# Score products of an attention and MLP kernel on four 64x64 corners of TensorE, in plain fp32 for all pairs

## The chip, the core and the metric

The kernel runs on one core of a Trainium2 chip. A core has five engines that work side by side, each with a queue of its own: TensorE (PE) for matmuls, VectorE (DVE), ScalarE (ACT), GpSimd (POOL), and SyncE (SP), which here only issues DMAs. PE reads its operands from SBUF, 128 partitions of on-chip memory, and writes to PSUM, also of 128 partitions; DVE and ACT read PSUM. The metric is the device time of one launch in microseconds.

## What is computed

Causal attention over 4 batches of 12 heads with 448 rows of 64, and on its result a two-layer MLP with 1792 tokens, 768 and 2048 wide:

```python
scores = q @ k.T / sqrt(64)                   # per head, 448 x 448
scores = np.where(upper_triangle, -1e9, scores)
attn = softmax(scores)
x = (attn @ v), heads side by side            # 1792 x 768
h = x @ w_in                                  # 1792 x 2048
g = np.where(h >= 1, h, np.where(h <= -1, 0, (h + 1) ** 2 / 4))
out = g @ w_out                               # 1792 x 768
```

q and k are large here (a spread of about 3.2), so that the softmax is sensitive to errors in the scores. The weights come as 8-byte floats and are narrowed on the chip.

## The kernel before

**Units of work.** Two heads form a pair: head 0 stands in SBUF partitions 0 to 63 and head 1 in 64 to 127. There are 24 pairs, `n_pair` 0 to 23, six in each batch. The 448 query rows of a head are seven tiles of 64, `i` = 0 to 6; by the causal mask tile `i` needs 64 (i+1) columns of keys.

**One pair.** `prep_pair` loads q and k (tile st) and transposes them on DVE to qs (L713). Scores go to PSUM tiles s (four of 128x512). DVE adds the mask and takes the row minimum of the negated scores (L884), ACT takes the exponential and its sum (L888), POOL or DVE and DVE make the reciprocal (L894 to L899), and one of three engines scales the row (`finish`, L768 to L772). `turn` transposes the rows on PE by a product with an identity (L785, 16 matmuls a pair) and ACT or DVE copies them to pt. PV (L913) multiplies them with v, on two halves of PE's columns, one for each head; its result is split into two rounded parts x (fp32r), which are the input of the first MLP product (L608, three passes: high with high, high with low, low with high).

**Scores, two ways.** Pairs 0 to 4 (`no < FLAT`) take q and k in plain fp32: `flat_scores` gives head 0 the corner of rows 0 to 63 and columns 0 to 63 of PE, head 1 the corner of rows 64 to 127 and columns 64 to 127 (L835, 14 matmuls a pair, of which each stands twice in the trace). Pairs 5 to 23 split q and k into a rounded part and the rest, tiles tt and ks (`copy_alts` L462 to L464, `sub_alts` L471 and L472), and compute in three fp32r passes: `last_scores` for tile 6 with both heads in one product by way of qb, a block diagonal of q (L845, 3 matmuls of 448 columns), and `wide_scores` for two tiles at once, each head on its half of PE's rows (L865, 18 matmuls; its tiles are as wide as the wider of the two).

**What sets the order.** Nothing is in program order. Each step is a task with the engines that may run it and a cost for each; `Plan.solve` ranks the tasks by due times, which `at()` and the tables of `steps_of_plan` give for PE, runs a model of the machine, and then moves tasks about by the seeds in `STEPS`, each of which stands for one random shift. The order of every engine's queue is what that model ends with. Loads of w_in (with their narrowing on ACT and DVE, L491 to L496, and splitting, L462 to L472) lie among the first ten pairs, w_out's after them. At the start PE runs `WARM` = 10 filling matmuls on zeros (L939) whose result nobody reads, and some more while pair 0 waits. After the last pair the second MLP product (L1028) runs alone on PE.

Of the kernel before, what the change touches and what calls it, by code (L numbers as in the profile page):

```python
# [2 lines left out]

# [30 lines left out]
class Task:  # L34
    def __init__(self, alts, prio):
        self.alts, self.prio = alts, prio
        self.deps, self.soft, self.allocs = set(), set(), []
        self.next = []
        self.mode = 0
        self.nom = self.moved = None  # L40
        self.lat = 1.6

# [5 lines left out]
class Plan:  # L48
# [8 lines left out]
    LANES = 8  # L57
    AHEAD = 12.0
# [88 lines left out]
    def solve(self):  # L147
# [4 lines left out]
        for ahead in (22.0,):  # L152
            for pen in (0.4,):
                self.AHEAD, self.PEN = ahead, {"DVE": pen, "ACT": 0.1}
# [29 lines left out]
    )  # L184

    def shake(self, seed):
# [8 lines left out]
        kind = rng.randrange(3)  # L195
# [15 lines left out]
    def run(self, dry=False):  # L211
        for t in self.tasks:
            t.reset()
        free, held, pe = {"SP": 0.56, "DVE": 0.63}, {}, Clock()
# [6 lines left out]
        while left:  # L221
# [21 lines left out]
            for prio, _, s, t in can:  # L243
                e0, c0, _, p0 = t.alts[0]
                c0 = 0.0 if e0 == "PE" else c0
                own = max(s, free.get(e0, 0.0) + queued.get(e0, 0.0), port if p0 else 0.0) + c0
                for a, (e, c, _, p) in enumerate(t.alts):
# [3 lines left out]
                    if a and st + c + queued.get(e, 0.0) + self.PEN.get(e, 0.0) >= own:  # L251
                        continue
                    chosen.setdefault(e, []).append(((st, prio), t, a, st, 0.0 if e == "PE" else c))
                queued[e0] = queued.get(e0, 0.0) + c0
            for e, cands in chosen.items():
                first = min(cands, key=lambda x: x[0])
                limit = first[3] + self.LOOK * first[4]
                key, t, a, st, _ = min((x for x in cands if x[3] <= limit and x[0][1] <= first[0][1]),
                                       key=lambda x: (x[0][1], x[0][0]))
                if best is None or key < best[0]:  # L260
                    best = (key, t, a, st)
# [85 lines left out]
def kernel(  # L347
# [9 lines left out]
    nc = tc.nc  # L357
# [27 lines left out]
    WARM = 10  # L385
# [6 lines left out]
        "tt": 2, "qs": 3, "ks": 2, "vr": 2, "pt": 2,  # L392
        **{f"p{i}": 1 for i in range(NI)}, "qb0": 1, "qb1": 1,
# [19 lines left out]
    open_pools(attn, "tt qs ks vr pt mn su")  # L413
# [17 lines left out]
    mask2 = early.tile([P, 3 * P], F32, name="mask2")  # L431
    nc.gpsimd.memset(mask2, 0.0)
    nc.gpsimd.affine_select(
        out=mask2[:, 2 * P:], in_=mask2[:, 2 * P:], pattern=[[-1, P]], compare_op=ALU.is_ge,
        fill=-1e30, base=0, channel_multiplier=1,
    )
# [6 lines left out]
    qb = [early.tile([P, 2, 2, T], F32R, name=f"qb{n}") for n in range(2)]  # L443
# [196 lines left out]
    S_AT = {6: 0.0, 5: 0.06, 4: 0.25, 3: 0.31, 2: 0.5, 1: 0.58, 0: 0.62}  # L640
# [19 lines left out]
    W_AT, W_T = 0.9, {6: 0.0, 5: 0.3, 4: 1.0, 3: 1.7, 2: 2.4, 0: 3.1}  # L660

    def at(n, kind, i):
        if n >= FLAT:
            t = starts[n] + W_AT
            if kind == "S":
                return starts[n] if i == 6 else t + 1e-4 * (i == 3)
# [8 lines left out]
        last = {6: 5, 5: 5, 4: 3, 3: 3}.get(i, 0)  # L675
        if kind == "T":
            return s_at(last) + LAG_T + 0.01 * (6 - i)
        return s_at(0) + LAG_T + LAG_V
# [6 lines left out]
    QS, KS, VR = {}, {}, {}  # L685
# [6 lines left out]
    def prep_pair(b, p, prio):  # L692
        no = b * HP + p
        flat = no < FLAT
        x = QS[b, p] = [buf("qs", [P, S]) for _ in range(2)]
        nat = []
        for g in range(2):
            t = buf("st", [P, ROW])
            first = None
            for i in range(2):  # L700
                row = (q, k)[g][b, 2 * p + i]
                for z in range(2):
# [3 lines left out]
                             dma(32 * 2 * S * 4, 230.0), 0.465, lat=1.25, early=no == 0, writes=[(t, 2 * i + z)], behind=loads[-1:] if first is None else ())  # L706
# [3 lines left out]
        ks = None if flat else buf("ks", [P, 2, S], F32R)  # L710
        qt = None if flat else buf("tt", [P, 2, S], F32R)
        for g, t in enumerate(nat):
# [4 lines left out]
            if flat:  # L717
                continue
# [5 lines left out]
        if flat:  # L724
            return
        bd, qd = plan.buf(f"qb{no % 2}", lambda: None), qb[no % 2]
        KS[b, p] = qt, ks, bd, qd
        if no in (FLAT, FLAT + 1):
            for z in range(2):
                task([("POOL", pool_ts(2 * T), lambda z=z: nc.gpsimd.memset(  # L730
                    qd[64 * z:64 * z + 64, :, 1 - z].bitcast(F32), 0.0), True)], prio, writes=[(bd, z)])
        for z in range(2):
            a = slice(64 * z, 64 * z + 64)
            task(copy_alts(lambda a=a, z=z: qd[a, :, z], lambda a=a: qt[a, :, S - T:].bitcast(F32), 2 * T, "POOL ACT DVE"),
                 prio, reads=[(qt, 0), (qt, 1)], writes=[(bd, 2 + z)])
# [15 lines left out]
    def pair(b, p, prio):  # L751
        n_pair = b * HP + p
        flat = n_pair < FLAT
        x, vr = QS[b, p], VR[b, p]
        qt, ks, bd, qd = KS.get((b, p), (None,) * 4)
# [4 lines left out]
        wide = [not flat and i < 6 for i in range(NI)]  # L760
        width = [T * ((i | 1 if wide[i] else i) + 1) for i in range(NI)]
# [14 lines left out]
        def turn(ii):  # L776
# [3 lines left out]
            def tr():  # L780
                for m, i in enumerate(ii):
                    for j in range(nb):
                        c = ((1 - m if wide[i] and nt > 1 else m) * nb + j) * P
                        k = min(P, S - j * P)
                        nc.tensor.transpose(t[:k, c:c + P], es[i][:, j * P:j * P + k], ident)  # L785
# [9 lines left out]
            def dst():  # L795
                if wide[lo] and nt > 1:
                    return pt[:, :2].rearrange("p i g q -> p g i q")
                if wide[lo]:
# [308 lines left out]
```

## Time and profile before

| | before |
|---|---|
| median of 3 runs | 633.13 us (631.77 to 633.73) |
| the profiled execution | 630.88 us |
| its span in the profile | 629.1 us |
| PE busy | 607.3 us (97%) |
| DVE busy | 467.3 us (74%) |
| ACT busy | 340.9 us (54%) |
| POOL busy | 208.5 us (33%) |

The profiled execution took 630.88 us, of which 629.1 are the span that the profile shows; 1.8 us lie around it. A busy PE counts from the start of a matmul to the end of its way through the array, and matmuls overlap, so the price of a matmul in a stream is the distance between starts and not its duration. A matmul in plain fp32 stands twice in the trace, as two records.

### The profile page before, as it was taken

To read this page: it belongs to the slowest core of one execution; us is meant where nothing else is said; L and a number is where in the kernel's file an instruction comes from. 1 tells how busy PE (TensorE), PEld (TensorE's weight loads), DVE (VectorE), ACT (ScalarE), POOL (GpSimd) and SP (SyncE) were. 2 spreads that over 40 slices of the span, in tenths; PEclk is the share of its full clock that TensorE was granted. 3 is DMA by queue.
4 is the path that set the end of the run, shared out by engine and by line. 5 is a ranking of instruction groups with operands and counts; after the bars stand their busy time and mean duration, and the time that the engine had idled before them with its cause. 6 is when DMAs were issued, how large, how long until landed. Compare 5 with 4: busy or idle time off the path is not lost.

```text
span 629.1 us, 11519 instructions
## 1 busy us (share of the span) xinstructions
PE 607.3 (97%) x3652; PEld 527.1 (84%) x3652; DVE 467.3 (74%) x1197; ACT 340.9 (54%) x851; POOL 208.5 (33%) x353
## 2 busy tenths in 40 slices
PE   7889999999999999999999999989999999999997
PEld 4455678797789798778798778979999999999997
DVE  4788898979996868976766619998766675665763
ACT  3888896748894546993554826845232322222320
POOL 3657765725661304681142606321101010110110
PEclk9999999999999999999999999999999999999999
DMA  8888789558868877668854119955423233424321
GB/s 212 235 198 214 188 244 278 143 165 244 252 192 272 245 241 228 167 204 244 260 160 162 31 51 324 329 177 191 118 84 118 72 118 83 131 68 118 105 83 64
DMA packets 96589, 110.33 MB, mean 175 GB/s; under 512 B 33552, under 2 KB 86288, under 8 KB 96528
## 3 DMA queue, kind: packets, MB, share of 16 engines
q1 hardware_dynamic: 96336, 109.15, 58.7%
q8 instruction: 29, 0.48, 0.3%
q10 hardware_dynamic: 192, 0.44, 0.2%
q14 instruction: 32, 0.26, 0.1%
HBM read 78.36 MB, written 31.20 MB: 174 GB/s over the span
## 4 chain that ended last, share of the span: by engine, by line
PE 73%; DMA 10%; DVE 7%; ACT 5%; issue 2%; POOL 1%; SPq 1%; ACTq 0%; DVEq 0%; POOLq 0%
PE h L608 21%; PE s L1028 16%; PE h L1028 8%; PE t L1028 8%; PE t L913 6%; DMA w<-in_moe_w_in_dram 6%; PE s L608 5%; PE t L785 5%; PE s L865 3%; ACT e L888 2%; DMA sr<-in_moe_w_out_dram 2%; DMA st<-in_q_dram 1%; DVE vv L621 1%; PE s L845 1%; DVE w L471 1%
## 5 line engine op out<-in xcount | busy, mean ns | idle before, releaser
L608 PE MATMUL h<-x,w 128*128 128x448 f32 x900 | 204.0, 372 | 2.7 <-DVE vv L621 2.2
L608 PEld LDWEIGHTS h<-x,w 128*128 128x128 f32 x900 | 162.3, 188 | 16.4 <-DVE vv L621 4.0
L462 ACT ACTIVATE hl<-z 128x896 fp32r<-128x896 f32 x56 | 53.5, 955 | 135.4 <-DVE z L471 93.9
L1028 PE MATMUL s<-w,hl 128*128 128x384 f32 x534 | 101.6, 335 | 3.1 <-DVE vv L621 3.1
L1028 PEld LDWEIGHTS s<-w,hl 128*128 128x128 f32 x534 | 93.5, 188 | 3.5 <-DVE vv L621 3.4
L888 ACT ACTIVATE e<-s,mn 128x128 f32<-128x128 f32 (+6 forms) x168 | 81.4, 496 | 16.0 <-DVE mn L884 11.8
L471 DVE TENSOR_TENSOR z<-z 128x128 f32<-128x128 f32 x196 | 54.4, 312 | 43.4 <-DMA z<-g_scratch 41.2
L884 DVE CUSTOM_DVE_ANT_0 s<-s,mask 128x128 f32<-128x128 f32 (+5 forms) x168 | 72.5, 468 | 8.9 <-PE s L835 4.9
L471 DVE TENSOR_TENSOR hl<-z,hl 128x896 fp32r<-128x896 f32 x54 | 60.4, 1126 | 15.8 <-ACT hl L462 15.7
L785 PE MATMUL t<-ident,e 128*128 128x128 f32 (+1 forms) x384 | 61.8, 279 | 5.6 <-ACT pt L818 1.8
L472 POOL TENSOR_TENSOR z<-z 128x128 f32<-128x128 f32 x28 | 12.6, 467 | 154.2 <-DMA z<-g_scratch 121.4
L785 PEld LDWEIGHTS t<-ident,e 128*128 128x128 f32 (+1 forms) x384 | 43.4, 139 | 20.5 <-ACT pt L816 3.0
L769 POOL TENSOR_SCALAR e<-e,su 128x256 f32<-128x256 f32 (+5 forms) x95 | 52.3, 556 | 24.0 <-DVE su L899 17.4
L618 ACT ACTIVATE r<-h,half 128x448 f32<-128x448 f32 x50 | 31.5, 635 | 45.9 <-PE h L608 44.4
L713 DVE STREAM_TRANSPOSE qs<-st 128x448 f32<-128x448 f32 x48 | 46.3, 968 | 11.2 <-DMA st<-in_q_dram 7.4
L816 ACT ACTIVATE pt<-t 128x256 f32<-128x256 f32 (+2 forms) x117 | 49.3, 445 | 8.3 <-PE t L785 7.9
L1028 PE MATMUL h<-w,hl 128*128 128x384 f32 x258 | 52.8, 335 | 0.0
L1028 PE MATMUL t<-w,hl 128*128 128x384 f32 x258 | 52.7, 335 | 0.0
L608 PE MATMUL s<-x,w 128*128 128x448 f32 x252 | 52.2, 364 | 0.4 <-DVE vv L621 0.4
L621 DVE TENSOR_TENSOR vv<-h,r 128x448 f32<-128x448 f32 x50 | 31.0, 620 | 26.7 <-ACT r L618 26.5
L913 PE MATMUL t<-pt,vr 128*64 128x448 f32 (+3 forms) x384 | 50.3, 391 | 0.5 <-ACT pt L816 0.4
L608 PEld LDWEIGHTS s<-x,w 128*128 128x128 f32 x252 | 46.9, 188 | 3.8 <-DVE vv L621 0.7
(103 smaller groups left out, 881.2 us busy)
## 6 DMA issues: line engine op xcount, KB each, us to landing
g_scratch<-r SPq DMA_DIRECT2D x64, 224.0 KB, 3.1
z<-g_scratch SPq DMA_DIRECT2D x56, 256.0 KB, 2.9
sr<-in_moe_w_out_dram SPq DMA_DIRECT2D x32, 384.0 KB, 4.4
w<-in_moe_w_in_dram SPq DMA_DIRECT2D x28, 384.0 KB, 4.8
w_scratch<-wn SPq DMA_DIRECT2D x56, 192.0 KB, 3.5
st<-in_q_dram SPq DMA_DIRECT2D x94, 108.0 KB, 3.4
st<-in_k_dram SPq DMA_DIRECT2D x94, 108.0 KB, 3.6
w<-w_scratch SPq DMA_DIRECT2D x50, 192.0 KB, 4.2
```

Source lines behind the costliest of these rows:

```text
L462: "ACT": ("ACT", act(n, 0.04), lambda: nc.scalar.activation(out=dst(), in_=src(), func=ACTF.Copy)),
L471: "DVE": ("DVE", dve(n), lambda: nc.vector.tensor_tensor(out=dst(), in0=x(), in1=y(), op=op), port),
L608: nc.tensor.matmul(out=h[:, :S], lhsT=wi[f][kk // K2][:, a, kk % K2 * P:(kk % K2 + 1) * P], rhs=x[:, c], start=(kk == 0 and n == 0), stop= ...
L621: task([("DVE", dve(S), lambda: nc.vector.tensor_tensor(out=y.tile, in0=h[:, :S], in1=r.tile, op=ALU.max))], g0, reads=[(h, 0), (r, 0)], w ...
L713: task([("DVE", 0.81, lambda g=g, t=t: nc.vector.transpose(out=x[g].tile.rearrange("p (r c) -> p c r", c=C), in_=bands(t[:, :32])))], prio ...
L769: ("POOL", pool_ts(n, 0.09), lambda: nc.gpsimd.tensor_scalar(out=ev(), in0=ev(), scalar1=sc(), scalar2=1.0, op0=ALU.mult, op1=ALU.mult), T ...
L785: nc.tensor.transpose(t[:k, c:c + P], es[i][:, j * P:j * P + k], ident)
L816: nc.scalar.activation(out=dst(), in_=src(), func=ACTF.Copy)
L884: task([("DVE", dve(n) + (0.05 if n < 384 else 0.02), lambda s=s, off=off, n=n, i=i: nc.vector.tensor_tensor_reduce(out=s[:, off:off + n], ...
L888: task([("ACT", act(n, 0.19), lambda s=s, off=off, n=n, i=i: nc.scalar.activation(out=es[i][:, :n], in_=s[:, off:off + n], func=ACTF.Exp, ...
L913: nc.tensor.matmul(out=o[64 * g:64 * g + 64, j * P:S], lhsT=vr[:k, j, g, :], rhs=pt[:k, 7 * j:5 * j + NI, g, :] if j < NJ - 1 else pt[:k, ...
L1028: nc.tensor.matmul(out=acc[x][:, :NO], lhsT=hl[:, a, i * P:(i + 1) * P], rhs=(hi, lo)[c](), start=(f == 0 and n == 0), stop=(f == KF - 2 a ...
```

## The change

All 24 pairs take their scores in plain fp32. `quads` computes a whole pair with 14 matmuls in two tasks, each with two s tiles. In the first s tile head 0 goes to partitions 0 to 63 and head 1 to 64 to 127, as in `flat_scores`; in the second tile they are crossed (`turned_`), so that all four corners of 64x64 are named in turn: head 0 straight, head 1 straight, head 0 crossed, head 1 crossed. Tile 6 (448 columns) is paired with tiles 5 and 0 (384 + 64), tiles 3 and 2 (256 + 192) with 4 and 1 (320 + 128). The crossed tiles are turned back by the transposes, whose identity is rotated by 64 columns for them (`SWAPPED`, `turners`). tt, ks, qb, mask2 and the wide and last products are gone. Around this the planner's costs, due times and seeds are new (`STEPS` has 150 seeds for 101), `qs` has four slots for three, the first two pairs use buffers of x (`head`), and `WARM` is 18.

```diff
-    TURNS_WIDE = ((6,), (5,), (4,), (3,), (2,), (0, 1))
     TURNS = ((6,), (5,), (4,), (2, 3), (0, 1))
     GROUPS = ((6, 5), (4, 3), (2, 1, 0))
-    GROUPS_WIDE = ((6,), (5, 4), (3, 2), (1, 0))
-    FLAT = 5
+    QUADS = ((6,), (5, 0)), ((3, 2), (4, 1))
+    SWAPPED = 5, 4, 1, 0
+    EVEN = 5
-    WARM = 10
+    WARM = 18
-        "tt": 2, "qs": 3, "ks": 2, "vr": 2, "pt": 2,
+        "qs": 4, "vr": 2, "pt": 2,
-    STEPS = (
-        1000008, 1000015, 1000095, 1000120, 1000197, 1000199, 1000222, 1000307, 1000343, 1000359, 1000388,
...
+        5000004, 5000005, 5000008, 5000014, 5000017, 5000026, 5000027, 5000036, 5000038, 5000043, 5000066,
...
-    ident = const.tile([P, P], F32, name="ident")
-    make_identity(nc, ident)
+    ident = const.tile([P, P + T], F32, name="ident")
+    make_identity(nc, ident[:, :P])
+    nc.gpsimd.tensor_copy(out=ident[:, P:], in_=ident[:, :T])
+    turners = ident[:, :P], ident[:, T:]
...
-                        nc.tensor.transpose(t[:k, c:c + P], es[i][:, j * P:j * P + k], ident)
+                        nc.tensor.transpose(t[:k, c:c + P], es[i][:, j * P:j * P + k], turners[i in SWAPPED])
...
-            y = (qt, ks)[g]
-            task(copy_alts(lambda y=y: y[:, 0], lambda g=g: x[g].tile, S, "ACT POOL DVE"),
-                 prio, reads=[(x[g], 0)], writes=[(y, 0)])
-            task(sub_alts(lambda y=y: y[:, 1], lambda g=g: x[g].tile, lambda y=y: y[:, 0].bitcast(F32), S, "DVE POOL"),
-                 prio, reads=[(x[g], 0), (y, 0)], writes=[(y, 1)])
...
+        def quads(slots):
+            ss = [buf("s", [P, 512]) for _ in slots]
+            queues, keys = [], []
+            for turned_, (s, tiles) in enumerate(zip(ss, slots)):
+                off = 0
+                queues.append([])
+                for i in tiles:
+                    place[i] = s, off
+                    keys.append((s, off))
+                    queues[-1].append((s, turned_, i, off))
+                    off += width[i]
+            def qk():
+                for step in zip_longest(*queues):
+                    for s, turned_, i, off in (y for y in step if y):
+                        for g in range(2):
+                            z, o = slice(64 * g, 64 * g + 64), 64 * (g ^ turned_)
+                            nc.tensor.matmul(out=s[o:o + 64, off:off + width[i]], lhsT=x[0][z, i * T:(i + 1) * T],
+                                             rhs=x[1][z, :width[i]], start=True, stop=True)
```

How the order moves, at two places. On SP, at the start, the rows of before (st, x: raw q and k; vr: v; w: raw w_in):

```order
L454 DMA st<-in_q_dram 32x864 x2
L454 DMA st<-in_k_dram 32x864 x2
L454 DMA vr<-in_v_dram 128x4x64 x2
L454 DMA w<-in_moe_w_in_dram 128x3x256
L454 DMA vr<-in_v_dram 128x4x64 x2
L454 DMA w<-in_moe_w_in_dram 128x3x256 x2
L454 DMA st<-in_q_dram 32x864 x2
```

and of the change:

```order
L463 DMA st<-in_q_dram 32x864 x2
L463 DMA st<-in_k_dram 32x864 x2
L463 DMA x<-in_q_dram 32x864 x4
L463 DMA x<-in_k_dram 32x864 x4
L463 DMA vr<-in_v_dram 128x4x64 x2
L463 DMA st<-in_q_dram 32x864 x3
L463 DMA st<-in_k_dram 32x864 x4
L463 DMA st<-in_q_dram 32x864
L463 DMA vr<-in_v_dram 128x4x64 x2
L463 DMA w<-in_moe_w_in_dram 128x3x256 x4
```

The q and k of the second and third pair have moved ahead of the first loads of w_in. On PE, among the pairs of the second batch, where PV of one pair (L913, L868) is followed by scores of a later one; before:

```order
L608 MATMUL h<-x,w 128x448 x60
L913 MATMUL t<-pt,vr 64x448 x2
L913 MATMUL t<-pt,vr 64x320 x2
L913 MATMUL t<-pt,vr 64x192 x2
L913 MATMUL t<-pt,vr 64x64 x2
L865 MATMUL s<-ks,tt 128x384 x6
L865 MATMUL s<-ks,tt 128x128 x6
L865 MATMUL s<-ks,tt 128x256 x6
L608 MATMUL h<-x,w 128x448 x12
L845 MATMUL s<-ks,qb_144 128x448 x3
```

and of the change:

```order
L868 MATMUL t<-pt,vr 64x64 x2
L820 MATMUL s<-qs 64x256 x2
L820 MATMUL s<-qs 64x320 x2
L820 MATMUL s<-qs 64x192 x2
L820 MATMUL s<-qs 64x128 x2
L820 MATMUL s<-qs 64x448 x2
L820 MATMUL s<-qs 64x384 x2
L820 MATMUL s<-qs 64x64 x2
L617 MATMUL h<-x,w 128x448 x15
L768 MATMUL t<-ident,e_130 128x128 x3
```

The wide products after a PV and the last tile's product among the MLP's matmuls have become one run of 14 small matmuls. Over the whole program DVE stands with 1211 instructions for 1197, ACT with 619 for 686, POOL with 247 for 351.

## Rows read from the trace of the kernel before

**Rows 1.** The page: busy time, share of the span and instructions of each engine.

```profile
PE 607.3 (97%) x3652; PEld 527.1 (84%) x3652; DVE 467.3 (74%) x1197; ACT 340.9 (54%) x851; POOL 208.5 (33%) x353
```

**Rows 2.** Stretches: length, busy us of PE, PEld, DVE, ACT, POOL; clock, DMA share, GB/s.

```profile
10.00:75.00 65.00, 58.45 (x418) 35.21 (x416) 52.49 (x181) 52.52 (x169) 40.07 (x73) 1.00 0.81 210
75.00:125.00 50.00, 47.36 (x278) 39.41 (x279) 46.07 (x107) 39.37 (x104) 31.60 (x41) 1.00 0.78 226
125.00:404.00 279.00, 276.77 (x1703) 231.81 (x1702) 213.75 (x578) 177.77 (x489) 112.07 (x187) 1.00 0.67 206
425.00:629.00 204.00, 200.59 (x1156) 200.26 (x1154) 132.03 (x293) 58.12 (x69) 15.80 (x28) 1.00 0.35 104
```

**Rows 3.** The chain of waits by line, from 10 to 125 us and from 125 to 425.

```profile
by line: DMA w<-in_moe_w_in_dram 30.5%; PE t L913 7.1%; PE h L608 6.6%; ACT e L888 4.8%; PE s L835 4.5%; PE t L785 4.3%; DMA st<-in_q_dram 4.1%; issue 3.8%; POOL e L769 3.3%; DVE qs L713 3.2%; ACT wn L491 3.2%; ACT pt L816 3.2%; DMA vr<-in_
...
by line: PE h L608 41.2%; PE s L608 10.1%; PE t L913 9.6%; PE t L785 8.4%; PE s L865 5.3%; DMA sr<-in_moe_w_out_dram 3.3%; issue 2.9%; DVE w L471 2.1%; ACT e L888 2.1%; DVE vv L621 2.0%; PE s L845 2.0%; DVE z L471 1.0%; DVE s L884 0.9%; DMA
```

**Rows 4.** PE's timeline from 208 us: start, us, line, operation, tiles, shapes, count.

```profile
208.19 4.12 PE L913 MATMUL t<-pt,vr 128*64 128x448 f32 x32
212.25 1.49 PE L865 MATMUL s<-ks,tt 64*128 64x384 f32 x18
213.67 0.87 PE L608 MATMUL h<-x,w 128*128 128x448 f32 x3
```

**Rows 5.** PE's timeline around the last tile's product of one pair.

```profile
198.48 0.78 PE L845 MATMUL s<-ks,qb 128*128 128x448 f32 x3
199.10 1.16 PE L608 MATMUL h<-x,w 128*128 128x448 f32 x5
```

**Rows 6.** The chain in order of time: start, us, what; a flat pair's scores, then PV.

```profile
20.91 3.01 PE s L835 x20
23.93 0.43 PE s L835 x4
24.37 1.97 PE t L913 x14
```

**Rows 7.** PE's timeline: two flat matmuls, and flat matmuls beside PV's last product.

```profile
20.84 0.59 PE L835 MATMUL s<-qs 64*64 64x448 f32 x2
...
26.08 0.27 PE L835 MATMUL s<-qs 64*64 64x64 f32 x1
26.17 0.23 PE L913 MATMUL t<-pt,vr 64*64 64x64 f32 x2
```

**Rows 8.** PE's timeline at the start; in brackets the idle time before and its releaser.

```profile
1.44 4.63 PE L939 MATMUL h<-ks 128*128 128x512 f32 x10 [1.44 <-DVE ks L932]
...
8.46 6.11 PE L835 MATMUL s<-qs 64*64 64x448 f32 x28 [2.39 <-DVE qs L713]
```

**Rows 9.** PE's timeline: four transposes and what starts after them.

```profile
161.85 0.62 PE L785 MATMUL t<-ident,e 128*128 128x128 f32 x4
162.40 1.49 PE L865 MATMUL s<-ks,tt 64*128 64x384 f32 x18
```

**Rows 10.** DVE's groups from 10 to 125 us: count, busy us, mean ns, idle before.

```profile
L884 DVE CUSTOM_DVE_ANT_0 s<-s,mask 128x384 f32<-128x384 f32 (+6 forms) x63 | 26.9, 458 | 6.3 <-PE s L835 4.9 <-ACT e L888 1.2 <-ACT qb L462 0.2
L713 DVE STREAM_TRANSPOSE qs<-st 128x448 f32<-128x448 f32 x21 | 20.4, 971 | 4.8 <-DMA st<-in_q_dram 3.4 <-PE s L835 1.0 <-DMA st<-in_k_dram 0.4
L496 DVE SCALAR_TENSOR_TENSOR wn<-w,wn 128x384 uint32<-128x384 uint32 x28 | 17.8, 647 | 0.1
L494 DVE TENSOR_SCALAR wn<-wn 128x384 uint32<-128x384 uint32 x28 | 11.3, 411 | 1.4 <-ACT wn L491 1.4
```

**Rows 11.** Instructions on tile qs: duration min/median/max in ns, first and last start.

```profile
L472 POOL TENSOR_TENSOR tt<-qs,tt x15: 1131/1152/1473, 49.1 to 341.9; 128x448 fp32r<-128x448 f32 x15
L471 DVE TENSOR_TENSOR ks<-qs,ks x14: 605/621/1010, 55.6 to 343.4; 128x448 fp32r<-128x448 f32 x14
```

**Rows 12.** PE's waits from 125 to 404 us: us in total, times, longest.

```profile
PE t L785 <- ACT pt L816: 1.0, 3, 0.5
...
PE t L785 <- ACT e L771: 0.2, 1, 0.2
```

More of the change, by code (lines that the diff above doesn't have):

```diff
@@ L41, in __init__ @@
         self.lat = 1.6
+        self.first = 0
     def reset(self):
@@ L57 @@
     LANES = 8
+    FREE = {"SP": 0.73, "ACT": 0.72, "DVE": 0.9, "POOL": 3.5}
     AHEAD = 12.0
@@ L151, in solve @@
         best = None
-        for ahead in (22.0,):
-            for pen in (0.4,):
-                self.AHEAD, self.PEN = ahead, {"DVE": pen, "ACT": 0.1}
+        for ahead in (14.0,):
+            for pen in (0.1,):
+                self.AHEAD, self.PEN = ahead, {"DVE": pen, "ACT": 0.1, "POOL": 12.0}
                 when = {t: t.nom for t in pe}
@@ L194, in shake @@
         part = rng.choice((0.03, 0.1, 0.3, 1.0))
-        kind = rng.randrange(3)
+        kind = rng.randrange(4)
+        if kind == 3:
+            for t in self.tasks:
+                if a <= t.begin <= z and t.moved is None and len(t.alts) > 1 and rng.random() < part:
+                    t.first = rng.randrange(len(t.alts))
+            return
         if kind == 2:
@@ L257, in run @@
                 limit = first[3] + self.LOOK * first[4]
-                key, t, a, st, _ = min((x for x in cands if x[3] <= limit and x[0][1] <= first[0][1]),
+                _, t, a, st, _, asked = min((x for x in cands if x[3] <= limit and x[0][1] <= first[0][1]),
                                        key=lambda x: (x[0][1], x[0][0]))
+                key = asked, t.prio if t.nom is None else t.nom
                 if best is None or key < best[0]:
@@ L430 @@
         )
[L431 to L436, printed above, removed]
     es = []
@@ L693, in prep_pair @@
         no = b * HP + p
-        flat = no < FLAT
-        x = QS[b, p] = [buf("qs", [P, S]) for _ in range(2)]
+        x = QS[b, p] = [head[2 + g] if no == 0 else buf("qs", [P, S]) for g in range(2)]
         nat = []
         for g in range(2):
-            t = buf("st", [P, ROW])
+            t = head[g] if no == 1 else buf("st", [P, ROW])
             first = None
@@ L705, in prep_pair @@
                              lambda row=row, z=z: bass.AP(row.tensor, row.offset + 32 * z, [[C * D, 32], [1, ROW]]),
-                             dma(32 * 2 * S * 4, 230.0), 0.465, lat=1.25, early=no == 0, writes=[(t, 2 * i + z)], behind=loads[-1:] if first is None else ())
+                             dma(32 * 2 * S * 4, 230.0 if no else 185.0), 0.465, lat=1.25 if no else 1.0, early=no == 0, writes=[(t, 2 * i + z)], behind=loads[-1:] if first is None else ())
                     first = first or one
@@ L759, in pair @@
         eb, done, turned = {}, [], []
-        wide = [not flat and i < 6 for i in range(NI)]
-        width = [T * ((i | 1 if wide[i] else i) + 1) for i in range(NI)]
+        width = [T * (i + 1) for i in range(NI)]
         def finish(i):
@@ L795, in dst @@
             def dst():
-                if wide[lo] and nt > 1:
-                    return pt[:, :2].rearrange("p i g q -> p g i q")
-                if wide[lo]:
-                    return rows(pt[:, lo & ~1:(lo | 1) + 1, 1 - lo % 2], nb)
                 if nt > 1:
@@ L826, in turn @@
                  prio, reads=[(t, 0)], writes=[(pt, i) for i in ii])
-        def flat_scores(i):
-            n, s = width[i], buf("s", [P, 512])
-            place[i] = s, 0
-            def qk():
-                for g in range(2):
-                    z = slice(64 * g, 64 * g + 64)
-                    nc.tensor.matmul(out=s[z, :n], lhsT=x[0][z, i * T:(i + 1) * T], rhs=x[1][z, :n],
-                                     start=True, stop=True)
-            return task([("PE", mm(4 * n, T, T, pair=True), qk)], prio, reads=[(x[0], 0), (x[1], 0)], writes=[(s, 0)]), 1
@@ L871, in pair @@
         place = {}
-        for group in GROUPS if flat else GROUPS_WIDE:
+        for group in GROUPS:
             for i in group:
@@ L903, in pair @@
             done.extend(group)
-            for ii in TURNS if flat else TURNS_WIDE:
+            for ii in TURNS:
                 if ii[0] not in turned and all(i in done for i in ii):
@@ L944 @@
     fill(WARM, -1.0)
+    head = [buf("x", [P, n]) for n in (ROW, ROW, S, S)]
     for b in range(B):
```

97 lines of the change are left out of this document (26 added, 71 removed), and 20 rows, old and new, of the table STEPS.

## The prediction, made before the change was run

> **What bounds the kernel now.** I read the page's busy shares first, then the engines' busy time by stretch, then the chain of waits of the same stretches, and last single matmul rows for prices. TensorE (PE) is busy 97% of the span [rows 1], but that is an average over three stages. In the last one (425 to 629 us, the second MLP product, which the change leaves alone) it is busy 200.6 of 204 us. From 125 to 404 us (pairs 10 to 23 with the first MLP product) it is busy 276.8 of 279. From 10 to 125 us (pairs 0 to 9) it is busy only 105.8 of 115, with VectorE (DVE) at 98.6 of 115, and at 46.1 of 50 from 75 us on, and the DMA engines' share near 0.8 [rows 2]. The chain says the same: from 125 to 425 us PE lines lead it (41% + 10% MLP, 10% PV, 8% transposes, 5% wide scores), from 10 to 125 us loads of w_in lead with 30%, and no PE line passes 8% [rows 3]. So a microsecond taken from PE after 125 us is a microsecond of the end; before 125 us it is worth something only as far as DVE, ACT and the loads follow.
>
> **The score products, the term that matters.** Prices are differences of starts, since the durations overlap. Before, one later pair (5 to 23) has 18 wide matmuls, 212.25 to 213.67 = 1.42 us [rows 4], and 3 of the last tile, 198.48 to 199.10 = 0.62 us [rows 5]: 2.04 us. A flat pair (0 to 4) in plain fp32 on two corners: 24 of its matmuls, that is widths 448 to 128 with 1728 columns, take from 20.91 to 24.37 = 3.46 us, 2.00 ns a column [rows 6]; the whole pair has 1792 columns: 3.6 us. The two corners do run at once: two matmuls of 0.59 us each lie inside 0.59 us [rows 7].
>
> After, each corner streams 448 columns in each of two groups, 896 in all. If four corners keep the pace that two keep, a pair costs 896 x 2.00 = 1.79 us. A second row gives nearly the same: PV runs in plain fp32 on two column halves, and its 32 matmuls (two pairs, 2048 columns) take 208.19 to 212.25 = 4.06 us [rows 4], 1.98 ns a column, 1.78 us. The best uninterrupted flat row (20 matmuls, 1600 columns, 3.01 us [rows 6]) gives 1.69. I take 1.78; the other end is that the corners go two and two, 3.6 us. That four do run at once no row shows. The nearest are two: in PV two column halves read the same rows at full pace, in the flat scores two row halves write the same tile at full pace; and at 26.08 to 26.2 us a corner of the score product streams while both corners of PV's last product are still under way [rows 7], three at once. And in the wide product two row halves write the same partitions of two s tiles at once: its 2 x 2304 columns at the last tile's pace (0.62 us for 1344 columns, 0.46 ns each [rows 5]) would take 2.1 us one after another, and they took 1.42. Each condition of the four corners is thus met somewhere, so I go with four.
>
> Here a rule of the Trainium skill speaks against the change: TensorEngine Tiling (Array Packing), section Gotcha 1: PSUM Pressure, says that different row tiles cannot access the same PSUM bank simultaneously. In the new product both row halves write each s tile. The flat rows did that already and overlapped fully [rows 7], so the trace disagrees for two corners; no run here shows it for four. By the rule the sum would be that of the first rival below.
>
> Saved on PE: later pairs 2.04 - 1.78 = 0.26 (0.35 by the best row), x19 = 4.9 to 6.7 us, of which the 14 pairs after 125 us are 3.6 to 4.9. Pairs 1 to 4: 3.6 - 1.8 = 1.8, x4 = 7.2 us. Entering and leaving the split array is paid once a pair in both kernels (the order keeps the 14 new matmuls of a pair mostly together), so I cost it at nothing; where groups stand apart it costs a few tenths, the 0.17 us by which flat and PV overran their columns.
>
> The first pair ran slower: 28 matmuls in 6.11 us from 8.46 to 14.57, 3.4 ns a column, and the ten filling matmuls before it went every 0.43 us or so (4.63 us for ten), the pace of the 1.2 GHz level, though the clock row reads 1.00 there [rows 2, 8]. PE had stood idle for 2.39 us between them. Now 18 fills reach from 1.44 to about 1.44 + 18 x 0.43 = 9.2 us without that gap. If the pace stays low the pair takes 896 x 3.4 = 3.0 us and ends at 12.2; if the 7.7 us of fills bring the upper level, as the 6 us of scores did before, it takes 1.8 and ends near 10.3. Against 14.57 that is 2.4 to 4.3 us; the 0.7 us of later start is in it. I take 3.
>
> PE work saved in all: 5 + 7 + 3 = 15 us (14.4 to 18.1).
>
> **What of it reaches the end.** After 125 us nearly all: 4 us (3.6 to 4.9). Before 125 us PE saves about 1.5 (five later pairs) + 7.2 + 3 = 11.7 us, and what is late next is DVE. Each pair needs seven mask-and-minimum passes on DVE (63 of them, nine pairs, took 26.9 us: 3.0 a pair, without the reading of their results) and two transposes of q and k of 0.97 [rows 10]: 4.9 us before any decoding, reciprocal or PSUM copy. PE needs 1.8 for scores, 2.03 for PV and, at four transposes in 0.55 us [rows 9], up to 2.2 for its sixteen: 6.0. The two run close together, so the gain must be shared with waits. Two things help: the order moves weight decoding behind the early pairs (when DVE ends the seventh pair's passes it has done 6 decodes and 14 transposes, before 10 and 17: 4 x (0.41 + 0.65) + 3 x 0.97 = 7.1 us less ahead of that point [rows 10]), and the first 8 us of loads are q and k instead of w_in. That decoding is not gone: it comes at pairs 8 and 9 (10 each), where DVE already was at 92%. So I count two thirds of 11.7, 8 us; the bounds are 3 (only the head) and 11.7.
>
> **The splitting that goes.** Nineteen pairs lose two subtractions each (1.15 us where POOL did them, 0.62 where DVE did [rows 11]), that is 24 to 44 engine-microseconds, and four copies each on top, and their score tiles become narrower. None of it is on the chain after 125 us; there PE's own waits for ACT, DVE and POOL are four groups, 1.0 us the largest and 0.2 the smallest, 2.0 in all [rows 12]. I count 1 us (0 to 2). What POOL loses is given back in part: by the order POOL takes 20 of the MLP's squares, and DVE gets 34 normalisations and 19 more PSUM copies while shedding 19 squares and 18 subtractions, which about balances. The smaller edits (rotated identity, one mask less, qs with four slots) have no instruction on the path.
>
> Sum: 4 + 8 + 1 = 13 us. The profiled execution took 630.88 us (span 629.1 and 1.8 around it), so 617.9; the median of the runs is 633.13, 2.2 higher, and I give the time on that footing: 633.1 - 13 = **620 us**. Ends: 633.1 - (4.9 + 11.7 + 2) = 614.5, and 633.1 - (3.6 + 3) = 626.5.
>
> **Rivals.** (1) The corners go two and two, because crosswise corners share an input row half with one neighbour and an s tile with another. Then a pair costs c = 3.6 us instead of 2.04. The 14 late pairs lose 14 x 1.56 = 21.8 us; the early five lose 7.8, less 2 of the head, two thirds of it, 3.9; the lighter elementwise work gives 1: 633.1 + 24.7 = 658 us, slower. By the same sum, 14 (c - 2.04) against 2/3 of 5 (2.04 - c) + 4 (3.6 - c) + 3, plus 1, it decides from c = 2.4 us on. For it: no row has four corners at once. Against: each condition taken alone is met at full pace [rows 4, 5, 7].
>
> (2) The early stretch does not follow: DVE and loads hold pairs 0 to 9 to the old 125 us but for the head. Then 3.6 to 4.9 + 3 = 626. For it: DVE at 92% from 75 to 125 us, w_in leading that chain, and a pair's scores that come in 1.8 us need 3.0 us of passes on DVE. Against: 10 to 75 us has DVE at 81%. The Trainium skill, on the same page under PSUM Bottleneck, warns that after a faster TensorE the PSUM copy may become the bottleneck; here it would give this rival's time.
>
> (3) The new order puts a softmax of a late pair behind DVE work that POOL did before, and PE waits where it did not: a normalisation on DVE queues behind one weight decode (1.06 us). At one such wait in each of the 14 late pairs 14 us are lost and the time is 634, no gain; at half of them, 627.
>
> **How the numbers follow.** Forecast 0.65, rival 2 0.14, rival 1 0.09, rival 3 0.12 (0.05 full, 0.07 half). A kernel change under 0.3% (1.9 us) can't be told from none. Faster: 0.65 + 0.14 + 0.07 - 0.01 = 0.85; same 0.04; slower 0.09 + 0.02 = 0.11. The range reaches from 610 (a few us below the lower end, since waits of the early stretch, 9 us in all, may shrink further) to 630, past rivals 2 and half of 3; rival 1 and the full rival 3 are left out.
>
> **What would show it.** In the changed profile a later pair's 28 score records (14 matmuls) should span 1.7 to 1.9 us, with four starts close together: 3 us or more means rival 1. The first pair's scores should end near 10 to 12 us. The first pair's PV, at 24.37 us before [rows 6], should start 3 to 5 us sooner, and w_in should leave the head of the early chain; if the MLP work begins to fill PE no sooner than at 75 us, that is rival 2. PE's busy share from 125 us on should stay at 99%; new waits for DVE there mean rival 3. The second MLP product should take its 204 us unchanged. The prediction fails if four corners don't overlap, or if the early stretch gives more than the head's own 12 us.

## The result, and the profile after

| | before | after |
|---|---|---|
| median | 632.45 us (630.62 to 633.73, 4 runs) | 613.56 us (612.28 to 615.45, 4 runs) |
| ratio | | 0.9706, 95% interval 0.9669 to 0.9742 |
| span of the profiled execution | 629.1 us | 613.6 us |

The change saves 18.9 us, 3%, where 13 were forecast. The page of after, busy time by engine, answers to [rows 1]:

```profile
PE 590.1 (96%) x3793; PEld 512.5 (84%) x3793; DVE 459.7 (75%) x1211; ACT 311.6 (51%) x784; POOL 186.6 (30%) x249
```

TensorE (PE) is busy 17 us less, close to the 15.5 us that the two spans differ by. The new score product is the first thing to look at. PE's timeline in after, one pair between MLP matmuls and PV (start, us, line, tiles, shapes, count):

```profile
186.22 1.75 PE L820 MATMUL s<-qs 64*64 64x448 f32 x28
187.90 2.10 PE L868 MATMUL t<-pt,vr 128*64 128x448 f32 x16
189.93 2.08 PE L617 MATMUL h<-x,w 128*128 128x448 f32 x9
```

From 186.22 to 187.90 is 1.68 us for a whole pair, 896 columns on each of four corners, against 2.04 of [rows 4, 5] and about 3.6 of [rows 6]. All four stream at once: on two corners the same pair takes 3.17 us (straight_late, below).

**Where the time came from.** Two states of the program can be compared. When pair 10's PV starts, both kernels have done ten PVs and 312 of the records of the first MLP product. When the first matmul of the second MLP product starts, the attention is over. The rows are those of two traces of the kernel before (the second is the run before_again below) and of after:

```profile
163.81 0.60 PE L913 MATMUL t<-pt,vr 128*64 128x448 f32 x2
...
417.32 0.69 PE L1028 MATMUL s<-w,hl 128*128 128x384 f32 x3
417.85 0.77 PE L608 MATMUL s<-x,w 128*128 128x448 f32 x3
...
422.22 0.79 PE L1028 MATMUL s<-w,hl 128*128 128x384 f32 x3 [3.08 <-DVE vv L621]
```

```profile
162.33 0.60 PE L913 MATMUL t<-pt,vr 128*64 128x448 f32 x2
...
416.79 0.69 PE L1028 MATMUL s<-w,hl 128*128 128x384 f32 x3
...
422.47 0.69 PE L1028 MATMUL s<-w,hl 128*128 128x384 f32 x1 [3.87 <-DVE vv L621]
```

```profile
155.90 0.60 PE L868 MATMUL t<-pt,vr 128*64 128x448 f32 x2
...
403.99 0.69 PE L984 MATMUL s<-w,hl 128*128 128x384 f32 x3
404.51 0.77 PE L617 MATMUL s<-x,w 128*128 128x448 f32 x3
...
406.77 0.77 PE L617 MATMUL s<-x,w 128*128 128x448 f32 x3
```

At these states the two kernels have not done quite the same work. At the first, after has the scores of 13 pairs behind it (364 records, 28 a pair) and before those of 12 (5 flat ones and 126 records of L865, 18 a pair), and after has the transposes of 12 pairs (192 records) for 11 (176). At the second, after has nine matmuls of the first MLP product still to do and before three. The score records up to the first state, L865 of before and L820 of after (start and end; length, busy PE and PEld with their counts):

```profile
0.00:163.80 163.80, 10.85 (x126) 9.21 (x126) 1.00 0.78 215
0.00:155.85 155.85, 23.16 (x364) 15.34 (x364) 1.00 0.75 211
```

The last column of the table is an estimate that allows for this. A pair's scores are taken at 1.68 us, its 16 transposes at 1.6 to 2.2 (four took 0.41 us from 191.98 us in after and 0.55 in [rows 9]), and six of those matmuls at 1.2 (three start over 0.61 us at 404.51). So 3.3 to 3.9 us are moved from the second stretch to the first, and 1.2 from the second to the third.

| stretch | before, two traces | after | less | for equal work |
|---|---|---|---|---|
| start to PV of pair 10 | 163.8, 162.3 | 155.9 | 6.4 to 7.9 | 9.7 to 11.8 |
| from there to the second MLP product | 253.5, 254.5 | 248.1 | 5.4 to 6.4 | 0.3 to 1.9 |
| from there to the end of the span | 211.8, 215.3 | 209.6 | 2.2 to 5.7 | 3.4 to 6.9 |

Nearly all of the gain is thus made before pair 10's PV and at the hand-over to the second product, and almost none between. The two kernels without the search (before_nosteps and after_nosteps below) bear this out. At their first state they have done equal work (12 pairs' scores, 176 transposes):

```profile
166.06 0.60 PE L913 MATMUL t<-pt,vr 128*64 128x448 f32 x2
...
424.65 0.51 PE L1028 MATMUL s<-w,hl 128*128 128x384 f32 x2
```

```profile
151.71 0.60 PE L868 MATMUL t<-pt,vr 128*64 128x448 f32 x2
...
407.30 0.69 PE L984 MATMUL s<-w,hl 128*128 128x384 f32 x3
```

That is 14.4 us less in the first stretch. The second is 3.0 us shorter and the third, with spans of 636.7 and 617.5 us, 1.9; with the nine matmuls by which their second states differ (1.8 us) these are 1.2 and 3.7. The first stretch is also the least steady: PV of pair 10 starts at 152.2 us in warm10 and at 159.0 in before_warm18, which take as long as after and before.

In the second stretch PE's shorter products turned into waits. By stretch, before and after (length; busy PE, PEld, DVE, ACT, POOL; granted clock, DMA share, GB/s):

```profile
163.80:417.30 253.50, 251.60 (x1523) 211.65 (x1522) 192.49 (x514) 160.05 (x433) 99.57 (x162) 1.00 0.67 207
155.85:403.95 248.10, 241.66 (x1556) 199.47 (x1556) 187.55 (x504) 142.20 (x378) 86.66 (x99) 1.00 0.73 222
```

PE stands idle 1.9 us of it in before and 6.4 in after. The 4.5 us between are about what the shorter scores of 12 pairs save, 12 x 0.36 = 4.3 us.

The third row of the table was in no step of the prediction. In before, PE waits at this hand-over for DVE's part of the last MLP tiles, 3.08 us in the first trace and 3.87 in the second. After has no such wait; its second product begins in turns with the last MLP matmuls, three groups of them for one. In the second trace of before the wait is followed by a fall of the clock to its lower level. The stretch after it, with the same columns:

```profile
419.00:429.00 10.00, 6.53 (x23) 6.53 (x24) 7.71 (x18) 2.99 (x5) 1.38 (x2) 0.66 0.41 131
```

The granted clock is 0.66 over these 10 us where the first trace has 1.00. The first trace is the exception: over a whole run the granted clock was 0.987 to 0.997 in all 36 runs of before beside the experiments, and 0.999 or 1.000 in the four of after. This is one reason why the runs of before spread, and why the medians differ by more than the two first spans.

At the start of after, PE's timeline, to be read beside [rows 8]:

```profile
1.44 6.92 PE L894 MATMUL h<-x 128*128 128x512 f32 x18 [1.44 <-DVE x L887]
8.29 1.75 PE L820 MATMUL s<-x 64*64 64x448 f32 x28
9.97 1.89 PE L894 MATMUL h<-x 128*128 128x512 f32 x7
13.34 0.98 PE L768 MATMUL t<-ident,e 128*128 128x128 f32 x7 [1.48 <-POOL e L752]
...
18.25 1.84 PE L868 MATMUL t<-pt,vr 128*64 128x448 f32 x12 [0.47 <-ACT pt L791]
```

The first pair's scores end at 9.97 us, before at 14.57, and its PV starts at 18.25, before at 24.37 [rows 6].

### The profile page after: what moved, and what is told of

Same layout as the page of the kernel before. It is cut to its first block, busy times and chain, and to the rows that moved or that the text cites. A ratio compares the mean times of both kernels' runs of the same rounds, so it can differ in the third digit from the quotient of the medians.

```text
span 613.6 us, 11591 instructions
## 1 busy us (share of the span) xinstructions
PE 590.1 (96%) x3793; PEld 512.5 (84%) x3793; DVE 459.7 (75%) x1211; ACT 311.6 (51%) x784; POOL 186.6 (30%) x249
## 4 chain that ended last, share of the span: by engine, by line
PE 47%; POOL 2%; DVE 1%; ACT 0%; issue 0%; POOLq 0%; ACTq 0%; DVEq 0%
PE s L984 17%; PE s L617 8%; PE h L984 8%; PE t L984 8%; PE h L617 3%; PE t L768 1%; PE t L868 1%; POOL r L633 1%; POOL r L634 1%; ACT e L843 0%; DVE vv L630 0%; DVE x L480 0%; DVE s L839 0%; PE s L820 0%; POOL su L849 0%
## 5 line engine op out<-in xcount | busy, mean ns | idle before, releaser
L471 ACT ACTIVATE hl<-z 128x896 fp32r<-128x896 f32 x49 | 46.7, 952 | 120.7 <-DVE z L480 96.5
L843 ACT ACTIVATE e<-s,mn 128x320 f32<-128x320 f32 (+6 forms) x168 | 78.4, 475 | 29.0 <-DVE mn L839 27.6
L480 DVE TENSOR_TENSOR hl<-z,hl 128x896 fp32r<-128x896 f32 x53 | 58.2, 1099 | 45.3 <-ACT hl L471 40.7
L839 DVE CUSTOM_DVE_ANT_0 s<-s,mask 128x320 f32<-128x320 f32 (+6 forms) x168 | 67.9, 445 | 6.7 <-PE s L820 3.2
L768 PE MATMUL t<-ident,e 128*128 128x128 f32 (+1 forms) x384 | 58.8, 278 | 11.7 <-ACT pt L791 4.7
L480 DVE TENSOR_TENSOR z<-z 128x128 f32<-128x128 f32 x199 | 56.5, 318 | 9.5 <-DMA z<-g_scratch 5.5
L868 PE MATMUL t<-pt,vr 128*64 128x448 f32 (+3 forms) x384 | 50.1, 391 | 3.7 <-ACT e L843 2.1
L633 POOL TENSOR_SCALAR r<-r 128x448 f32<-128x448 f32 x20 | 36.2, 1808 | 52.7 <-DVE vv L630 51.9
L868 PEld LDWEIGHTS t<-pt,vr 128*64 128x64 f32 (+1 forms) x384 | 23.9, 135 | 32.8 <-issue 19.9
L984 PEld LDWEIGHTS h<-w,hl 128*128 128x128 f32 x258 | 45.5, 188 | 0.0
```

The source lines that it names most:

```text
L471: "ACT": ("ACT", act(n, 0.04), lambda: nc.scalar.activation(out=dst(), in_=src(), func=ACTF.Copy)),
L480: "DVE": ("DVE", dve(n), lambda: nc.vector.tensor_tensor(out=dst(), in0=x(), in1=y(), op=op), port),
L633: nc.gpsimd.tensor_scalar(out=r.tile, in0=r.tile, scalar1=1.0, scalar2=1.0, op0=ALU.min, op1=ALU.mult)
L839: task([("DVE", dve(n) + (0.05 if n < 384 else 0.02), lambda s=s, off=off, n=n, i=i: nc.vector.tensor_tensor_reduce(out=s[:, off:off + n], ...
L843: task([("ACT", act(n, 0.19), lambda s=s, off=off, n=n, i=i: nc.scalar.activation(out=es[i][:, :n], in_=s[:, off:off + n], func=ACTF.Exp, ...
L868: nc.tensor.matmul(out=o[64 * g:64 * g + 64, j * P:S], lhsT=vr[:k, j, g, :], rhs=pt[:k, 7 * j:5 * j + NI, g, :] if j < NJ - 1 else pt[:k, ...
```

## The experiments

All variants keep the changed kernel's queues in the same order unless said otherwise; only what an entry of a queue emits is edited. Times are medians; the differences are to 613.56 for variants of after. The kernel before, run beside them, had 633.4, 632.0 and 633.2 us.

**Two corners in the late pairs (straight_late, pairs 10 to 23), and in the early pairs (straight_early, `n_pair >= 10` for `n_pair < 10`).** The transposes of these tiles take the plain identity.

```diff
-   ... turners[i in SWAPPED]
+   ... turners[i in SWAPPED and n_pair < 10]
...
-   z, o = slice(64 * g, 64 * g + 64), 64 * (g ^ turned_)
+   z, o = slice(64 * g, 64 * g + 64), 64 * (g ^ (turned_ if n_pair < 10 else 0))
```

> The changed kernel with the same order of all queues, but pairs 10 to 23 put the second score tile of each group on the straight corners too, so that only two of the four corners are used (their transposes take the plain identity). My theory: the gain of a later pair is that four corners stream at once, and after pair 9 TensorE's time is the end's time. A pair then has 1792 columns on each corner instead of 896: 1.66 us becomes 3.0 to 3.6, so 14 x 1.4 to 1.9 = 20 to 27 us more, 634 to 641 us against 613.6, slower than the kernel before (632.5). Rival: the gain came from the new order and the lighter elementwise work, and TensorE has slack: under 8 us more, below 622.

> The same edit for pairs 0 to 9 alone. TensorE's work grows by 10 x 1.4 to 1.9 = 14 to 19 us. My theory, as predicted: in the early stretch two thirds of TensorE's time reach the end, 9 to 13 us more: 623 to 627 us. Rival a: early TensorE time is free, because VectorE and the loads set the pace: under 5 us more. Rival b: all of it reaches the end: 14 to 19 us, 628 to 633.

Measured: straight_late 626.97 us (625.75 to 630.11), ratio to before 0.9913 (0.9883 to 0.9943), 13.4 us more; straight_early 625.36 us (624.10 to 626.24), 0.9877 (0.9847 to 0.9907), 11.8 us more. PE's timeline of straight_late, the same pair as above:

```profile
187.66 3.24 PE L820 MATMUL s<-qs 64*64 64x448 f32 x28
190.83 0.60 PE L868 MATMUL t<-pt,vr 128*64 128x448 f32 x2
```

The pair takes 3.17 us on two corners, 1.49 more, so the crossed corners are what halves it. But 14 x 1.49 = 20.9 us on PE became 13.4 at the end, a share of 0.64, and 10 x 1.49 = 14.9 became 11.8, 0.79. The intervals leave some 3 us in each difference, so 0.64 is good to about 0.15 and 0.79 to 0.2: the late share is short of 1, but the two can't be told apart. For the late pairs neither my theory (20 to 27 us) nor its rival (under 8) came true: they don't pass on all. The early ones came out as expected. PE's waits in after, 110 to 386 us (us in total, times, longest), and in straight_late, 130 to 400 us, show where the rest went:

```profile
PE h L617 <- DVE vv L630: 2.5, 4, 1.1
PE t L768 <- DVE e L755: 2.4, 5, 0.6
PE t L768 <- POOL e L752: 2.3, 2, 1.7
PE t L768 <- ACT pt L791: 0.6, 1, 0.6
```

```profile
PE h L617 <- DVE vv L630: 2.1, 3, 1.0
PE s L820 <- DVE qs L718: 0.2, 1, 0.2
PE t L768 <- POOL e L752: 0.2, 1, 0.2
```

After waits some 8 us there (two more rows have 0.3 each), where before waited 2.0 in a stretch of like length [rows 12] and straight_late 2.5; the longer scores fill these waits. With the shorter scores the other engines have come close enough to be waited for.

**The crossed tiles last (inorder).**

```diff
-   for step in zip_longest(*queues):
-       for s, turned_, i, off in (y for y in step if y):
+   for step in queues:
+       for s, turned_, i, off in step:
```

> The changed kernel, but the second group of a pair issues both straight tiles (256 and 192 columns) before the two crossed ones (320 and 128), instead of in turn; the first group's order is the same as before. If TensorE holds a queue for each corner and looks past a matmul whose corner is busy, a pair costs 1.66 us as it did and the time is 613.6 +- 2. If matmuls start in the order of the program, the first crossed one waits until the second straight one starts, 256 columns in two passes or 0.43 us later: a pair costs 2.0 to 2.1 us, 24 x 0.4 = 10 us more on TensorE and 7 to 10 at the end, 621 to 624.

Measured: 615.31 us (614.32 to 618.25), 0.9727 (0.9693 to 0.9762). PE's timeline of inorder:

```profile
187.08 1.79 PE L820 MATMUL s<-qs 64*64 64x448 f32 x28
188.80 2.10 PE L868 MATMUL t<-pt,vr 128*64 128x448 f32 x16
```

A pair costs 1.72 us, 0.04 more and not 0.43. In the second group of this pair the program has the 192 columns wide matmuls of the straight tile ahead of the 320 wide ones of the crossed tile. The matmuls of L820 that were under way from 188.08 to 188.30 us (durations in ns; first and last start):

```profile
L820 PE MATMUL s<-qs x8: 376/402/472, 187.9 to 188.2; 64*64 64x256 f32 x4, 64*64 64x320 f32 x4
```

All four records of 320 columns had started by 188.2 us and none of 192. A matmul for a free corner thus starts although the one ahead of it in the program waits for a busy corner. Naming the corners in turn is worth 24 x 0.04 = 1 us on PE; the medians stand 1.8 us apart, too little to tell from none.

**The fills (warm10; before_warm18 with 18 for 10), and a second trace of before (before_again).**

```diff
-   for _ in range(times):
+   for _ in range(10 if times == WARM else times):
```

> The changed kernel with 10 filling matmuls at the start for 18, the order otherwise the same. My theory: without them the first pair's scores run at the lower pace again, 3.0 us for 1.7, and the first PV, at 18.2 us, comes 1 to 3 us later; two thirds of it reach the end: 1 to 2 us, 614.5 to 616. Rival: the fills are nothing but a delay of the first scores, which now start when the operands land, and the time falls by up to 0.5 us.

> The kernel before with 18 filling matmuls at the start for 10, the order otherwise the same. If the first pair's slow scores (6.1 us, 3.4 ns a column) are the idle gap before them and reach the end, the clock stands at its upper level when they start, they take 3.3 us, and the time falls by 1 to 3 us, to 629 to 631. Rival: as in warm10 against the changed kernel, no difference: the gain at the head is not the fills'.

> The kernel before, for a second trace. In the first one the clock rose to its upper level at 14.3 us, in the traces of the changed kernel and its variants between 4.7 and 7.5. If that is the idle gap between fills and scores, it rises at 14 us again; if it is where the chip happens to look, at some other time, and the first pair's 28 matmuls take 3.3 to 6.1 us accordingly.

Measured: warm10 613.83 us (611.89 to 614.56, 5 runs), 0.9699 (0.9670 to 0.9728), as fast as after; before_warm18 632.63 us (629.46 to 634.92), 0.9996 (0.9969 to 1.0022), as slow as before; before_again 633.92 us. The number of fills is thus worth nothing that these runs can tell, which would show some 2 or 3 us. The traces speak against my price for the head by the clock. In warm10 the scores ran at the full pace after ten fills and 1.80 us of idling, and they started when q and k had landed and DVE had transposed them:

```profile
1.44 4.08 PE L894 MATMUL h<-x 128*128 128x512 f32 x10 [1.44 <-DVE x L887]
7.31 1.75 PE L820 MATMUL s<-x 64*64 64x448 f32 x28 [1.80 <-DVE x L718]
```

before_again and before_warm18 show what held the first pair as well. PE's timeline of before_again, then of before_warm18:

```profile
8.57 4.32 PE L835 MATMUL s<-qs 64*64 64x448 f32 x20 [3.08 <-DVE qs L713]
13.28 0.44 PE L835 MATMUL s<-qs 64*64 64x128 f32 x4 [0.39 <-ACT e L888]
14.76 0.33 PE L835 MATMUL s<-qs 64*64 64x64 f32 x4 [1.04 <-ACT e L888]
```

```profile
8.61 3.17 PE L835 MATMUL s<-qs 64*64 64x448 f32 x20
12.53 0.43 PE L835 MATMUL s<-qs 64*64 64x128 f32 x4 [0.75 <-ACT e L888]
13.47 0.33 PE L835 MATMUL s<-qs 64*64 64x64 f32 x4 [0.51 <-ACT e L888]
```

With 18 fills the first 20 records are quicker, and the last two tiles still come at 12.5 and 13.5 us: they wait for ACT's exponentials. The flat pair takes seven s tiles and PSUM has four slots for them, so the last three wait until a row has been read. The new product packs a pair into four. The first trace of before has this wait in a later flat pair:

```profile
40.93 0.54 PE L835 MATMUL s<-qs 64*64 64x192 f32 x4 [1.49 <-ACT e L888]
```

**The splitting, with its waits (split_back) and without (load_only).** Pairs 5 to 23 do it again into tiles that nobody reads, behind each transpose of q (g = 0) and k on DVE. load_only reads the constant mask for `x[g].tile`, so that the added work waits for no transpose.

```diff
+   if g == 0:
+       nc.gpsimd.tensor_scalar(out=y[:, 0], in0=x[g].tile, scalar1=1.0, scalar2=1.0, op0=ALU.mult, op1=ALU.mult)
+       nc.gpsimd.tensor_tensor(out=y[:, 1], in0=x[g].tile, in1=y[:, 0].bitcast(F32), op=ALU.subtract)
+   else:
+       nc.scalar.activation(out=y[:, 0], in_=x[g].tile, func=ACTF.Copy)
+       nc.vector.tensor_tensor(out=y[:, 1], in0=x[g].tile, in1=y[:, 0].bitcast(F32), op=ALU.subtract)
```

> The changed kernel, and for pairs 5 to 23 the splitting of q and k is done again into spare tiles that nobody reads: after each transpose a copy and a subtraction of 448 columns, q's on GpSimd (0.57 + 1.15 us), k's on ScalarE and VectorE (0.58 + 0.62), in those queues at that place; all else in the same order. It adds 19 x 1.7 = 33 us to GpSimd, 11 to ScalarE, 12 to VectorE. As predicted, this work was off the path: 0 to 2 us more, 613.6 to 615.6. Rival: since TensorE's time reaches the end only by 0.6 to 0.8 (the two straight runs), the other engines are close to the bound, and the freed elementwise work made part of the gain: 4 to 8 us more, 617.5 to 621.5.

> split_back again, but the added copies and subtractions read the constant mask and not q and k, so that they keep their engines as long but wait for nobody: 19 x 1.7 us on GpSimd, 19 x 0.6 on ScalarE, 19 x 0.62 on VectorE, at the same places of the queues. Theory: the 42 us of split_back were queues that stood behind a transpose not yet done (22 us of GpSimd's waits and 19 of ScalarE's were for it), and the work itself costs 0 to 4 us: 613.6 to 618. Rival: the order leaves these engines no room, and the work itself costs 20 us or more.

Measured: split_back 655.87 us (653.84 to 661.02), 1.0370 (1.0304 to 1.0437), 42.3 us more; load_only 635.70 us (632.45 to 639.02), 1.0052 (1.0021 to 1.0083), 22.1 us more. Both theories failed, and load_only's rival held: the order leaves these engines no room. About half of the 42 us was queues behind a transpose not yet done; the work by itself costs 22. PE's waits from 60 us to the end of the attention, load_only and then after:

```profile
PE t L778 <- POOL e L762: 7.3, 5, 1.9
PE h L618 <- DVE vv L631: 6.7, 10, 1.3
PE t L778 <- DVE e L765: 6.3, 6, 1.9
PE t L778 <- ACT pt L801: 2.3, 3, 1.4
```

```profile
PE h L617 <- DVE vv L630: 2.9, 5, 1.1
PE t L768 <- POOL e L752: 2.6, 3, 1.7
PE t L768 <- DVE e L755: 2.4, 5, 0.6
PE t L768 <- ACT pt L791: 2.0, 2, 1.4
```

A busy share of 30% on POOL had not meant room: PE's waits for POOL's normalisations (L762 here, L752 in after) rose from 2.6 to 7.3 us, and those in these rows for DVE from 5.3 to 13.0. Which engine's part of the added work (34 us on POOL, 14 on DVE, 11 on ACT) costs how much, no run separates. The order was not planned with this work in it, so 22 us is not what the splitting cost in before, only a proof that it is not free in a tight order.

**The prices of before in the order of after (old_pe, old_prices).** Pairs 0 to 4 on two corners, and for the others

```diff
-   for step in zip_longest(*queues):
+   steps = list(zip_longest(*queues))
+   for step in steps + steps[-1:] * (n_pair >= 5 and 3 in slots[0]):
```

old_prices does the splitting of split_back too.

> old_prices without the splitting: the changed kernel in its own order, pairs 0 to 4 on two straight corners (3.17 us a pair for 1.68), pairs 5 to 23 with the 192 and 128 columns wide tiles of the second group computed twice (0.33 us more, about 2.0). From the straight runs, with 0.79 of a microsecond of TensorE reaching the end in pairs 0 to 9 and 0.64 after: 5.9 + 1.3 + 3.0 = 10 us more, 622 to 626. Rival: TensorE's prices alone made the gain of 18.9 us: 630 to 633.

> The changed kernel in its own order but at about the prices of before: pairs 0 to 4 on the two straight corners (3.17 us a pair), pairs 5 to 23 with the narrow half of the second group computed twice (about 0.33 us more, 2.0 a pair), and the splitting of q and k done again as in split_back. If the gain of 18.9 us is these prices alone, the time is 630 to 633. From the two straight runs I expect less: 5 x 1.49 x 0.79 = 5.9, 5 x 0.33 x 0.79 + 14 x 0.33 x 0.64 = 4.3, the splitting 1: 613.6 + 11 = 623 to 626, so that 7 to 8 us of the gain are the new order's (first loads, wait ahead of the second MLP product).

Measured: old_pe 623.59 us (622.55 to 626.05), 0.9860 (0.9817 to 0.9904), 10.0 us more, as expected. old_prices 659.38 us, 1.0415 (1.0363 to 1.0467): it carries split_back's waiting queues, 3.5 us on top of them, and tells nothing about the question it was made for. PE's price alone is thus 10 of the 18.9 us in this order. It is a low figure for the flat pairs of before: old_pe gives them 3.17 us and four s tiles, where before took 3.46 for 24 of its 28 records [rows 6] and had seven tiles to place.

**Both kernels without the search (after_nosteps, before_nosteps).**

```diff
-   for seed in self.STEPS:
+   for seed in ():
```

> The changed kernel without its 150 seeds: the order is that of the planner's first ranking. With before_nosteps it tells whether the gain is the product's or the search's. My theory: the product's prices hold in any order, so this kernel is 10 to 20 us faster than before_nosteps. Rival: the gain is a luckier search, and the two come within 5 us of each other.

> The kernel before without its 101 seeds, the pair to after_nosteps: slower than 632.5 by whatever the search was worth, say 640 to 660 us; after_nosteps is expected 10 to 20 us below it, by the rival within 5.

Measured: after_nosteps 620.72 us (619.37 to 622.03), 0.9803 (0.9757 to 0.9848); before_nosteps 638.90 us (638.32 to 643.37), 1.0113 (1.0048 to 1.0178). They stand 18.2 us apart, as the two tuned kernels do. The search was worth 6 to 7 us in each; the gain is not a luckier set of seeds. Due times, tables and planner rules still differ between the two.

## Why the prediction held, and which steps did not

The forecast added 4 us late, 8 early and 1 for the splitting. For equal work the traces give 0.3 to 1.9, 9.7 to 11.8 and, at a hand-over that was in no term, 3.4 to 6.9; the splitting cannot be read from them. The time came out inside the range with one term too high and two too low, and that is in part luck.

**Four corners at once: right.** This was the hinge, priced from two flat corners and PV's two halves: 1.78 us a pair, 1.69 at best; it measured 1.68. The rule that spoke against it (the Trainium skill, TensorEngine Tiling (Array Packing), Gotcha 1: PSUM Pressure) does not show here: both row halves write each s tile and the pair still takes about half of what two corners take (3.17). Rival 1 is out. At 1.68 for 1.78 a pair saved 0.10 us more than forecast, 2.4 us of PE over 24 pairs and by the shares of the straight runs 1.7 of the 6 that the forecast lacked.

**The early stretch: more than forecast, partly for another reason.** Forecast 8 us of 11.7 saved on PE; measured 9.7 to 11.8, and 14.4 without the search. That is the whole saving and not two thirds of it, though straight_early puts the share at 0.79, good to 0.2. Rival 2 is out. The head's 3 us were laid to the clock, and the fills proved to be worth nothing measurable. The first pairs' gain is also the four s slots, a wait that stood in the code before (seven tiles, four slots) and that I passed over because the first trace puts the first pair's whole delay down to its slow matmuls.

**The late stretch: too high.** Forecast 4 us; for equal work 0.3 to 1.9 were gained from pair 10's PV to the second product. The saving on PE was there (0.36 us a pair), and the step that failed is that all of it reaches the end. The rule that a microsecond of PE after 125 us is one of the end was read from the kernel before, with PE busy 276.8 of 279 us; in the changed kernel it is 0.64. PE's busy share was to stay at 99% and fell to 97 (241.7 of 248.1 us), with waits for DVE and POOL that before did not have. That is rival 3 in part: a loss of 4.5 us where it had put 7 or 14.

**The splitting off the path, 0 to 2 us: not confirmed.** The 2.0 us of PE's waits [rows 12] were the measure of a finished order and not of the work's price: the search had placed that work where it hurt least. load_only's 22 us show that the room is small in the order of after.

**Nothing at the hand-over: wrong.** The sum ended with the attention, and the second product was to take its time unchanged. The wait ahead of it, 3.1 to 3.9 us in before, is seen in the trace and was taken for fixed. Its end is worth 3.4 to 6.9 us, with the clock's fall at the upper end.

What stays open: PE's prices explain 10.0 of the 18.9 us. The trace of old_pe ends its hand-over as after does (210.0 us from there to the end for 209.6), so the hand-over comes on top with 3.4 to 6.9. That leaves 2 to 5.5 us for the splitting that went, the loads moved ahead and the s slots, and how they share it no run shows. Why the order of after has no wait at the hand-over is open too. In an order planned as a whole these can't be put back one by one, as split_back showed.

## What to carry to other kernels

A product with 64 rows and 64 output columns uses a quarter of the array; with a second output tile crossed to the other partitions (and a rotated identity to turn it back for free) it can use all of it, and plain fp32 then costs less than three rounded passes with their splitting. Count PSUM tiles as well as columns. Where an order was searched, small waits on an engine say how well its work was placed and not what the work costs, and work added to a fixed order can reach the end although its engines have idle time (22 us for 34 on POOL, 14 on DVE and 11 on ACT). Before two orders are compared at a state of the program, count what each has already done.

## What the runs showed of the hardware

- Four corners of 64x64 in plain fp32, each with matmuls of its own: 28 records of a pair in 1.68 us, and 3.17 on two corners, a factor of 1.89.
- Matmuls of different corners do not start strictly in the order of the program: with both straight tiles ahead of both crossed ones a pair took 1.72 us, and the crossed 320 columns started before the straight 192 that stood ahead of them.
- After the same ten fills the first pair's scores ran at either level of PE's clock. In before_again, after a gap of 3.08 us, the granted clock was 0.50 from 8.50 to 10.00 us. In the first trace of before, after 2.39 us, the 28 records took 6.11 us [rows 8], the lower pace, though the clock row reads 1.00 there. In warm10, after 1.80 us, they ran at the upper level from the first.
- At the hand-over idle times of 3.87 us (before_again) and 3.86 us (before_warm18) were each followed by the lower level, 0.66 on average over 10 us; idle times of 3.08 us (before) and 2.02 us (before_nosteps) were not.
